# A fused linear-attention and SwiGLU block on one core: the last tile's output split at column 512, and one SwiGLU unit made by halves

## The chip, the core and the metric

The kernel runs on one core of one Trainium2 chip. Time is device time in microseconds (us). The kernel before was run three times: 268.52, 268.66 and 268.88 us, median 268.66. A profiled execution of the same kernel shows every engine: TensorE (PE for its products, PEld for its weight loads, which can overlap the products), VectorE (DVE), ScalarE (ACT), GpSimd (POOL) and SyncE (SP), whose queue issues all the transfers of this kernel.

## The reference

A layer norm of `x` (2048 tokens of 640 features) feeds two branches whose results are added to `x`: a linear attention with a softmax feature map (32 heads of 20 features), and a SwiGLU block of width 1536.

```python
def _A_ref(x, wqkv, w_phi, wo):
    qkv = (x @ wqkv).reshape(B, S, 3, H, Dh).transpose(2, 0, 3, 1, 4)
    q, k, v = qkv[0], qkv[1], qkv[2]
    pq = einsum("bhsd,hdf->bhsf", q, w_phi)
    pk = einsum("bhsd,hdf->bhsf", k, w_phi)
    phi_q = concatenate([softmax(pq), softmax(-pq)], axis=-1)
    phi_k = concatenate([softmax(pk), softmax(-pk)], axis=-1)
    kv = einsum("bhsf,bhsd->bhfd", phi_k, v)
    z  = einsum("bhsf->bhf", phi_k)
    num = einsum("bhqf,bhfd->bhqd", phi_q, kv)
    den = einsum("bhqf,bhf->bhq", phi_q, z)[..., None] + 1e-6
    return (num / den).transpose(0, 2, 1, 3).reshape(B, S, D) @ wo

def _B_ref(x, w1, w3, w2):
    return (silu(x @ w1) * (x @ w3)) @ w2

return x + _A_ref(layernorm(x), ...) + _B_ref(layernorm(x), ...)
```

All arrays are bfloat16.

## The kernel before

Tokens are taken in 16 tiles of 128. The normed input stands transposed in `xnT` (five chunks of 128 features by 2048 tokens). Matrix products accumulate in PSUM, in banks of 512 float32 columns: a pool of six single banks, from which each user takes the next in turn, and one pair. The whole order of work is written out by hand: within one engine's queue, instructions run in the order of the program's text.

The work has three stages.

- A start, in which tiles are loaded, normed and transposed, V is computed, and the weights of the feature map are fused into `wkphi`. Nine of the 48 SwiGLU units are made here, the first two of them in halves by `glu_half`.
- A K stage over 16 tiles: `phi_unit` (products `pk`, L342), the accumulation of `kv` (L485), and two SwiGLU units for a tile, one for the first.
- A Q stage, a loop over t = 0 to 19. While t < 16 it makes `phi_unit` (products `pq`, L342) of tile t. For t = 0 to 3 it makes the last eight SwiGLU units, two for each t, by `fill(2)`. From t = 4 it makes `out_unit` for tile t - 4 and stores the result. `r_unit` (products `pr`, L520) and the division for tile t - 2 stand behind that.

A SwiGLU unit (`glu_unit`, L444) covers 128 of the 1536 hidden features and 512 tokens: five products of 512 columns into the bank `gp` (weights `w1`), five into the bank `up` (weights `w3`). Then ACT takes a Tanh of `gp` (L455), and DVE makes `gs` (L472) and the product for `hT` (L475). `glu_half` (L461) makes one half of a bank, 256 tokens, with five products of 256 columns. `glu_done` starts the Tanh and returns the function that makes the two DVE products.

`out_unit` (products `acc`, L583) makes the output of one tile: 17 rows of weights, 12 from `w2` and 5 from `wo`, each a product with 128 tokens as the stationary operand. For the first 15 tiles the two column halves, 320 each, alternate product by product, and the result is stored by one transfer. For the last tile (`last` is set, t = 19) the columns are done in two parts, one after the other: all 17 products of the first part, its eviction on DVE with the residual added (`result`, L592), its store on SP, and the same for the second part.

Behind the loop stands a branch on every engine (L882): where a bound on the weights isn't met, the attention is made again with the maximum taken off. With these inputs the branch jumps over that part, to the closing barrier (L929), in which SP checks one semaphore after another.

Of the kernel before, what the change touches and what calls it, by code (L numbers as in the profile page):

```python
# [12 lines left out]
def kernel(  # L13
# [24 lines left out]
    _, S, D = A_x.shape  # L38
# [28 lines left out]
    def bank(name, dt=f32):  # L67
        n = 512 if dt == f32 else 1024
        return psum.tile([P, n], dt, name=name, tag="bank")

    def pair(name):
        return psum2.tile([P, 2, 512], f32, name=name, tag="pair")
# [5 lines left out]
    w1 = one.tile([P, KD, F], bf, name="w1")  # L78
    w3 = one.tile([P, KD, F], bf, name="w3")
# [48 lines left out]
    def ld(dst, src):  # L128
        nc.sync.dma_start(out=dst, in_=src)
# [9 lines left out]
    with tc.manual_schedule():  # L139
# [193 lines left out]
        def tile_of(t):  # L333
            return slice(t * P, (t + 1) * P)

        def by_token(cols, w, name, cut, ps=None):

            ps = ps or [bank(name), bank(name)]
            for c in range(KD):
                for i in range(2):  # L340
                    a, b = (0, cut) if i == 0 else (cut, D)
                    nc.tensor.matmul(  # L342
                        ps[i][:, 0 : b - a],
                        xnT[:, c, cols],
                        w[:, c, a:b],
                        start=(c == 0),
                        stop=(c == KD - 1),
                        skip_group_check=True,
                    )
            return ps  # L350
# [45 lines left out]
        def phi_unit(t, w, name, exps=exps, cols=None):  # L396

            ps = by_token(cols or tile_of(t), w, name, CH)
            dst = phi[:, t % 4]
            exps(ps, dst)  # L400
            rows = dst.rearrange("p c g f -> p (c g) f")[:, :, 0:60].rearrange(
                "p a (i d) -> p a i d", d=Dh
            )
            sk = work.tile([P, 2 * NCH, 3], f32, name="sk")
            nc.vector.reduce_sum(out=sk[:], in_=rows, axis=AX.X)  # L405
            rk = work.tile([P, 2 * NCH, 3], f32, name="rk")
            nc.vector.reciprocal(out=rk[:], in_=sk[:])  # L407
            nc.gpsimd.tensor_mul(  # L408
                out=rows, in0=rows, in1=rk[:, :, :, None].to_broadcast([P, 2 * NCH, 3, Dh])
            )  # L410
# [28 lines left out]
        def glu_unit(sc, fi, banks=None):  # L439

            gp, up = banks or (bank("gp")[:], bank("up")[:])
            for ps, w in ((gp, w1), (up, w3)):
                for c in range(KD):
                    nc.tensor.matmul(  # L444
                        ps,
                        w[:, c, fi * P : (fi + 1) * P],
                        xnT[:, c, sc * 512 : (sc + 1) * 512],
                        start=(c == 0),
                        stop=(c == KD - 1),
                    )  # L450
            return glu_done(sc, fi, gp, up)

        def glu_done(sc, fi, gp, up):
            th = work.tile([P, 512], f32, name="th")
            nc.scalar.activation(out=th[:], in_=gp, func=AF.Tanh, scale=0.5)  # L455
            return lambda: glu_product(sc, fi, gp, up, th)

        def glu_half(i, w, sc, fi, ps):

            for c in range(KD):  # L460
                nc.tensor.matmul(  # L461
                    ps[:, i * 256 : (i + 1) * 256],
                    w[:, c, fi * P : (fi + 1) * P],
                    xnT[:, c, sc * 512 + i * 256 : sc * 512 + (i + 1) * 256],
                    start=(c == 0),
                    stop=(c == KD - 1),
                    skip_group_check=True,
                )

        def glu_product(sc, fi, gp, up, th):  # L470
            gs = work.tile([P, 512], bf, name="gs")
            nc.vector.scalar_tensor_tensor(  # L472
                out=gs[:], in0=th[:], scalar=1.0, in1=gp, op0=ALU.add, op1=ALU.mult
            )
            nc.vector.scalar_tensor_tensor(  # L475
                out=hT[:, 4 * sc : 4 * sc + 4, fi, :],
                in0=gs[:].rearrange("p (t s) -> p t s", t=4), scalar=0.5,
                in1=up.rearrange("p (t s) -> p t s", t=4), op0=ALU.mult, op1=ALU.mult,
            )

        def kv_unit(t, v1, acc, first, last):

            for c in range(NCH):
                b, i = divmod(c, 6)
                nc.tensor.matmul(  # L485
                    acc[:, b, VC * i : VC * i + 1 + Dh * HC[c]],
                    phi[:, t % 4, c].rearrange("p g f -> p (g f)"),
                    v1[:, c, 0 : 1 + Dh * HC[c]],
                    start=(first and i == 0),
                    stop=last,  # L490
                    skip_group_check=True,
                )
# [77 lines left out]
        def residual(rows):  # L570
            xr = work.tile([P, D], bf, name="xr")
            ld(xr[:], x2[rows, :])
            return xr

        def out_unit(h, ocols, xr, last=None):

            acc = [bank("acc"), bank("acc")]
            rows = [(h[:, k], w2[:, k]) for k in range(KF)]
            rows += [(oT[:, k, ocols], wo[:, k]) for k in range(KD)]
            res = work.tile([P, D], bf, name="res")  # L580

            def product(j, ps, a, b):
                nc.tensor.matmul(  # L583
                    ps[:, 0 : b - a],
                    rows[j][0],
                    rows[j][1][:, a:b],
                    start=(j == 0),
                    stop=(j == len(rows) - 1),
                )

            def result(ps, a, b):
                nc.vector.tensor_tensor(  # L592
                    out=res[:, a:b], in0=ps[:, 0 : b - a], in1=xr[:, a:b], op=ALU.add
                )

            if last is None:
                parts = [(acc[i], i * HD, (i + 1) * HD) for i in range(2)]
                for j in range(len(rows)):
                    for part in parts:
                        product(j, *part)  # L600
                for part in parts:
                    result(*part)
                return res
            for part in ((acc[0], 0, 384), (acc[1], 384, D)):
                for j in range(len(rows)):
                    product(j, *part)
                result(*part)
                a, b = part[1:]
                ld(out2[last, a:b], res[:, a:b])
# [13 lines left out]
        def flag_unit():  # L623
# [12 lines left out]
        glu = [  # L636
            (sc, fi) for cols in (range(0, 4), range(4, KF)) for sc in range(NSC) for fi in cols
        ]

        def fill(n):  # L640
            for _ in range(n):
                glu_unit(*glu.pop(0))()
# [171 lines left out]
        ps = by_token(tile_of(15), wv, "pv", CH)  # L814
# [6 lines left out]
        acc = pair("pkv")  # L821
# [24 lines left out]
        for t in range(NST + 4):  # L846
            if t < NST:
                phi_unit(t, wqphi, "pq")
            if t < 2:
                kv_unit(turns[t - 2], vaug[:, turns[t - 2]], acc, False, t == 1)  # L850
                if t == 1:
                    kv_done([acc[:, 0], acc[:, 1]])
                    ld(w2, B_w2.rearrange("(c p) d -> p c d", p=P))
            if t < 4:
                fill(2)
            else:
                last = tile_of(NST - 1) if t == NST + 3 else None
                res = out_unit(hT[:, t - 4], tile_of(t % 4), xr, last)
            if 2 <= t < NST + 2:
                r_unit(t - 2)  # L860

            if 3 <= t < NST + 3:
                xr = residual(tile_of(t - 3))
            if 4 <= t < NST + 3:
                ld(out2[(t - 4) * P : (t - 3) * P, :], res[:])
            if t < NST:
                phi_transposed(t)
            if 2 <= t < NST + 2:
                o_transposed(t - 2)
            if t < 4:  # L870
                norm_unit(wqphi, 1, t)
            if t == 4:
                ld(listed[:], norms[:])
                ld(flat, listed[:].rearrange("p g -> (p g)").partition_broadcast(1))
            if t == 6:
                flag_unit()
            if t == 8:
                ok = nc.values_load(flag[0:1, 0:1], min_val=0, max_val=1)
# [3 lines left out]
    with tc.If(ok == 0):  # L882
# [4 lines left out]
        with tc.For_i(0, NST, 1) as t:  # L887
# [3 lines left out]
            acc = pair("pkv")  # L891
# [42 lines left out]
```

## Time and profile before

| what | us |
|---|---|
| median of three runs | 268.66 (268.52 to 268.88) |
| the profiled execution's own time | 268.62 |
| its span, first to last instruction | 266.8 |
| PE busy | 262.0 |
| products of `out_unit`, 320 columns, 299 ns each | 51.3 and 22.8 |
| products of the SwiGLU units, 512 columns, 379 ns each | 57.0 (`up`) and 55.8 (`gp`) |
| weight loads of PEld, 98 ns each | 167.7 in all |
| last eviction on DVE starts | 263.79 |

The duration of a product is from its start to its end, modelled; products overlap, so the step from the start of one to the start of the next is read from groups in the timeline, which give the start of the first and the length of the whole. A few product records are missing from the trace, so that a group can show fewer than it had. In the timeline, "SPq" is SP's queue: the time in which it issues a transfer. "To landing" is the time from that issue to the last semaphore update of the transfer. Register, branch and semaphore instructions are not counted as busy; their times stand in the answers by line.

### The profile page before, as it was taken

How to read it: one execution, taken by the hardware profiler on the slowest of the kernel's cores; microseconds unless marked ns; L12 is line 12 of the kernel's file. 1: busy time of each engine (PE TensorE's matmuls, PEld its weight loads, DVE VectorE, ACT ScalarE, POOL GpSimd, SP SyncE). 2: the span in 40 equal slices, each digit the busy share in tenths (PEclk: the TensorE clock that was granted, in tenths of full speed). 3: DMA queues.
4: the chain of work that ended last, by engine and by line, in shares of the span. 5: the costliest groups of instructions: out<-in, count | busy, mean ns of one | idle time of the engine just before them, and what ended most of it. 6: DMA issues, size and time to landing. Idle time of an engine off the chain costs nothing.

```text
span 266.8 us, 5294 instructions
## 1 busy us (share of the span) xinstructions
PE 262.0 (98%) x1979; PEld 167.7 (63%) x1997; DVE 195.0 (73%) x363; ACT 114.8 (43%) x348; POOL 91.1 (34%) x88
## 2 busy tenths in 40 slices
PE   8999999999999999999999999999999999999995
PEld 7766565655555555555555555677777777777773
DVE  4779984398766777779998699976877777776341
ACT  5784444744466666344556665422222222221000
POOL 5052520055333333333444333333344444333000
PEclk9999999999999999999999999999999999999999
DMA  6998856976000000060000098455655555556931
GB/s 192 248 245 185 125 118 160 333 136 119 0 0 2 0 1 3 1 176 0 0 2 0 0 270 179 114 142 144 130 128 133 149 130 128 137 147 130 155 98 55
DMA packets 69373, 29.46 MB, mean 110 GB/s; under 512 B 56287, under 2 KB 67935, under 8 KB 69344
## 3 DMA queue, kind: packets, MB, share of 16 engines
q1 hardware_dynamic: 69344, 29.08, 46.9%
q8 instruction: 17, 0.28, 0.4%
q14 instruction: 12, 0.10, 0.2%
HBM read 13.14 MB, written 2.63 MB: 59 GB/s over the span
## 4 chain that ended last, share of the span: by engine, by line
PE 98%; issue 0%; DVE 0%
PE acc L583 28%; PE up L444 19%; PE gp L444 18%; PE pq L342 8%; PE pk L342 8%; PE pv L342 6%; PE pr L520 2%; PE pkv L485 2%; PE pv L299 2%; PE pf L428 1%; PE idle L202 1%; PE pst L288 1%; PE g L461 1%; PE v L299 1%; PE gp L461 0%; PE up L461 0%
## 5 line engine op out<-in xcount | busy, mean ns | idle before, releaser
L408 POOL TENSOR_TENSOR phi<-phi,rk 128x1320 bf16<-128x1320 bf16 x32 | 77.2, 2412 | 129.0 <-DVE rk L407 102.3
L444 PEld LDWEIGHTS <-w 128*128 128x128 bf16 x460 | 43.4, 98 | 47.9 <-DMA w<-in_B_w_dram 0.2
L405 DVE TENSOR_REDUCE sk<-phi 128x66 f32<-128x1320 bf16 x32 | 48.8, 1526 | 26.7 <-ACT phi L371 25.7
L444 PE MATMUL up<-xnT,w 128*128 128x512 bf16 x227 | 57.0, 379 | 0.3
L444 PE MATMUL gp<-xnT,w 128*128 128x512 bf16 x215 | 55.8, 378 | 0.7
L583 PE MATMUL acc<-reg_v,reg_h 128*128 128x320 bf16 (+2 forms) x384 | 54.9, 299 | 0.0
L342 PEld LDWEIGHTS <-xnT 128*128 128x128 bf16 x440 | 41.7, 98 | 19.3 <-DMA xnT<-reg_h 0.5
L371 ACT ACTIVATE phi<-pq 128x360 bf16<-128x360 f32 (+2 forms) x96 | 24.8, 366 | 57.7 <-issue 34.6
L583 PEld LDWEIGHTS <-reg_h 128*128 128x128 bf16 x384 | 37.4, 98 | 14.4
L455 ACT ACTIVATE th<-gp 128x512 f32<-128x512 f32 x47 | 28.4, 603 | 27.9 <-PE gp L444 25.7
L475 DVE SCALAR_TENSOR_TENSOR reg_h<-gs,up 128x512 bf16<-128x512 bf16 x47 | 32.3, 688 | 4.8
L472 DVE SCALAR_TENSOR_TENSOR gs<-th,gp 128x512 bf16<-128x512 f32 x47 | 30.9, 658 | 4.3 <-ACT th L455 4.3
L371 ACT ACTIVATE phi<-pk 128x360 bf16<-128x360 f32 (+2 forms) x96 | 24.9, 370 | 20.0 <-PE pk L342 20.0
L592 DVE TENSOR_TENSOR res<-acc,xr 128x320 bf16<-128x320 f32 (+2 forms) x32 | 14.2, 484 | 19.0 <-PE acc L583 19.0
L583 PE MATMUL acc<-reg_w,reg_v 128*128 128x320 bf16 (+2 forms) x160 | 24.5, 299 | 0.0
L342 PE MATMUL pk<-wkphi,xnT 128*128 128x360 bf16 (+1 forms) x160 | 24.3, 299 | 0.0
L342 PE MATMUL pq<-wqphi,xnT 128*128 128x360 bf16 (+1 forms) x160 | 24.3, 299 | 0.0
L407 DVE RECIPROCAL rk<-sk 128x66 f32<-128x66 f32 x32 | 18.1, 567 | 3.2
L583 PEld LDWEIGHTS <-reg_v 128*128 128x128 bf16 x160 | 15.7, 98 | 6.1
L342 PE MATMUL pv<-reg_w,xnT 128*128 128x360 bf16 x120 | 17.4, 299 | 0.0
L228 DVE BATCH_NORM_STATS2 st<-reg_h 128x6 f32<-128x320 bf16 x32 | 13.4, 477 | 4.1 <-DMA reg_h<-in_A_x_dram 4.1
L541 DVE TENSOR_TENSOR o__77<-pr,den 128x360 bf16<-128x360 f32 (+1 forms) x32 | 14.2, 486 | 0.6
(82 smaller groups left out, 162.4 us busy)
## 6 DMA issues: line engine op xcount, KB each, us to landing
w<-in_B_w_dram SPq DMA_DIRECT2D x2, 1280.0 KB, 6.3
xr<-in_A_x_dram SPq DMA_DIRECT2D x16, 160.0 KB, 2.4
out_dram<-res SPq DMA_DIRECT2D x15, 160.0 KB, 1.8
reg_h<-in_A_x_dram SPq DMA_DIRECT2D x6, 320.0 KB, 4.7
reg_v<-in_B_w_dram SPq DMA_DIRECT2D x1, 1920.0 KB, 9.2
w<-in_B_w_dram SPq DMA_DIRECT2D x4, 320.0 KB, 4.4
reg_w<-in_A_wqkv_dram SPq DMA_DIRECT2D x5, 160.0 KB, 3.1
reg_w<-in_A_wo_dram SPq DMA_DIRECT2D x1, 800.0 KB, 7.2
```

What stands on the lines that cost most here:

```text
L342: nc.tensor.matmul(ps[i][:, 0 : b - a], xnT[:, c, cols], w[:, c, a:b], start=(c == 0), stop=(c == KD - 1), skip_group_check=True,)
L371: nc.scalar.activation(out=dst[:, c0 : c0 + n, g, 0:k], in_=p.rearrange("p (c f) -> p c f", c=n), func=AF.Exp, scale=1.0 - 2.0 * g,)
L405: nc.vector.reduce_sum(out=sk[:], in_=rows, axis=AX.X)
L407: nc.vector.reciprocal(out=rk[:], in_=sk[:])
L408: nc.gpsimd.tensor_mul(out=rows, in0=rows, in1=rk[:, :, :, None].to_broadcast([P, 2 * NCH, 3, Dh]))
L444: nc.tensor.matmul(ps, w[:, c, fi * P : (fi + 1) * P], xnT[:, c, sc * 512 : (sc + 1) * 512], start=(c == 0), stop=(c == KD - 1),)
L455: nc.scalar.activation(out=th[:], in_=gp, func=AF.Tanh, scale=0.5)
L472: nc.vector.scalar_tensor_tensor(out=gs[:], in0=th[:], scalar=1.0, in1=gp, op0=ALU.add, op1=ALU.mult)
L475: nc.vector.scalar_tensor_tensor(out=hT[:, 4 * sc : 4 * sc + 4, fi, :], in0=gs[:].rearrange("p (t s) -> p t s", t=4), scalar=0.5, in1=up.r ...
L541: nc.vector.tensor_mul(out=o_[:, t % 2, Dh * h0 : Dh * h1].rearrange("p (h d) -> p h d", d=Dh), in0=p3[:, :, 0:20], in1=den[:, h0:h1, None ...
L583: nc.tensor.matmul(ps[:, 0 : b - a], rows[j][0], rows[j][1][:, a:b], start=(j == 0), stop=(j == len(rows) - 1),)
L592: nc.vector.tensor_tensor(out=res[:, a:b], in0=ps[:, 0 : b - a], in1=xr[:, a:b], op=ALU.add)
```

## The change

Two places are edited. The last tile's two parts become columns 0 to 512 and 512 to 640, in place of 0 to 384 and 384 to 640; both stores are still issued by SP. In the Q stage, at t = 0, the second of the two SwiGLU units is made by a new function, which makes each of the two banks in two halves of 256 tokens: 20 products of 256 columns with 20 weight loads, in place of 10 products of 512 columns with 10 weight loads. The order of all other instructions on every engine is the same; PE's program has 20 instructions more.

```diff
+        def glu_by_halves(sc, fi):
+
+            gp, up = bank("gp")[:], bank("up")[:]
+            for ps, w in ((gp, w1), (up, w3)):
+                for i in range(2):
+                    glu_half(i, w, sc, fi, ps)
+            glu_done(sc, fi, gp, up)()
+
...
-            for part in ((acc[0], 0, 384), (acc[1], 384, D)):
+            for part in ((acc[0], 0, 512), (acc[1], 512, D)):
                 for j in range(len(rows)):
                     product(j, *part)
                 result(*part)
...
             if t < 4:
-                fill(2)
+                fill(1)
+                if t == 0:
+                    glu_by_halves(*glu.pop(0))
+                else:
+                    fill(1)
             else:
```

The new function's `glu_half` is the one of the start, unchanged. Lines of the changed kernel from `glu_by_halves` on are 8 to 12 higher than those of the kernel before: `product` is L591, `result` L600, the branch L894 and the barrier L941.

## The prediction

> **What bounds the kernel now.** I read three views in this order: the busy table of the page, the chain that ended last in order of time, and the timeline of the last 8 us.
>
> ```profile
> PE 262.0 (98%) x1979; PEld 167.7 (63%) x1997; DVE 195.0 (73%) x363; ACT 114.8 (43%) x348; POOL 91.1 (34%) x88
> ```
>
> ```profile
> 146.46 1.08 PE gp L444 x5
> 147.54 1.08 PE up L444 x5
> ...
> 254.51 9.26 PE acc L583 x68
> 263.77 0.02 issue
> 263.79 0.42 DVE res L592
> ```
>
> TensorE (PE) is busy for 262.0 of 266.8 us, and the chain is PE from the first product to 263.77. In the Q stage one unit follows the other without a hole: gp and up of the first SwiGLU unit of t = 0 take 1.08 us each. So whatever PE does more or less in this stage goes straight to the end; nothing covers it. After the last product there is a tail in which PE no longer counts.
>
> ```profile
> 258.97 2.11 PE L583 MATMUL acc<-reg_v,reg_h 128*128 128x384 bf16 x12
> 261.73 1.47 PE L583 MATMUL acc<-reg_v,reg_h 128*128 128x256 bf16 x12
> 261.93 0.56 DVE L592 TENSOR_TENSOR res<-acc,xr 128x384 bf16<-128x384 f32 x1 [2.01 <-PE acc L583]
> 263.04 0.71 PE L583 MATMUL acc<-reg_w,reg_v 128*128 128x256 bf16 x5
> 263.79 0.42 DVE L592 TENSOR_TENSOR res<-acc,xr 128x256 bf16<-128x256 f32 x1 [1.30 <-PE acc L583]
> ```
>
> ```profile
> 264.24 0.33 SPq L129 DMA_DIRECT2D out_dram<-res  x1
> ```
>
> ```profile
> L882 SPq EVENT_SEMAPHORE  x4: 17/17/17, 265.1 to 265.4; - x4
> L882 PEldq COMPARE_BRANCH  x1: 3617/3617/3617, 261.6 to 261.6; - x1
> L882 SPq COMPARE_BRANCH  x1: 53/53/53, 264.6 to 264.6; - x1
> ```
>
> The tail is: eviction (264.21), issue of the second store on SP (264.24 to 264.57), SP's branch around the fallback (264.63), then a row of semaphore checks on SP, 60 to 80 ns apart without a hole, to 265.97, and the closing barrier. In the trace's records by semaphore, the check on PE stands at 265.85 and was met since 265.33; the check on the second store stands at 265.91 and its last part had landed at 265.76. Neither held SP. So the end follows SP's last issue by 2.55 us, and that issue follows the last eviction. The slacks, 0.51 us for PE's branch and 0.15 us for the store, are what a change can use up.
>
> **The change, part by part.**
>
> *The unit by halves.* Ten 512-column products become twenty of 256. A run of five 512-column products takes 1.08 us, 216 ns each. 256 columns: the last part's first to thirteenth product start 263.04 - 261.73 = 1.31 us apart, 12 steps, 109.2 ns. The half products at the start of the kernel (L461) step by the same. 20 x 109.2 - 10 x 216 = +24 ns on PE. All twenty weight loads lie under the products, as they do there. The buffers, the Tanh and the two DVE products are the same, released when the last half of gp or up is done; that moves with those 24 ns only. No range is needed: the same shape with the same operands stands in the trace.
>
> *The last tile on PE.* 17 x 384 + 17 x 256 columns become 17 x 512 + 17 x 128. Before: the first part steps by (261.73 - 258.97) / 17 = 162.4 ns. After: 17 x 216 = 3.67 us, then 16 steps of 128 columns to the last product's start. The nearest row for 128 columns at full clock is the transposes of one tile early on:
>
> ```profile
> 12.79 0.44 PE L288 MATMUL pst<-ident,reg_h 128*128 128x128 bf16 x5
> 13.07 0.71 PE L461 MATMUL gp<-xnT,w 128*128 128x256 bf16 x5
> ```
>
> Five in 0.28 us, 56 ns each. The last product so starts at 258.97 + 0.024 + 3.67 + 16 x 0.056 = 263.565 against 263.480 before: +85 ns with the halves. It lasts 219 ns (median of the 128-column row of L288) in place of 273: -54 ns. Bounds: 54 ns (a third of the 162.4 of 384 columns) to 109 (no gain over 256 columns, +0.85 us); I take 56, since the 63-column products of L520, each with its own weight load, run eleven in 0.33 us, 30 ns each, so no weight load holds them at more than that.
>
> The Trainium skill, TensorE: Matmul & The Clock Gate, Back-to-back issue gap, speaks against this: it gives about 81 ns for 128 columns in a stream of weight loads and products, and 131 for 512. By that the sixteen steps would take 16 x 25 = 0.40 us more than by the row, an estimate. The trace disagrees at both ends that it has (216 ns at 512 columns, 30 ns at 63).
>
> *The evictions.* 256 columns took 424 ns, 384 took 558: 1.05 ns a column. So 128 columns take 290 (-134 ns) and 512 take 692. The first part's last product starts at 262.45 and ends 0.38 later at 262.83 (378 ns is the 512-column mean), its eviction ends at 263.56, and the last product at 263.78: DVE is free by 0.22 us. Were it not, the last eviction would wait for the rest.
>
> *The stores on SP.* The first store, 128 KB, is issued at 263.58 to 263.92 in place of 262.52; the second is ready when the last eviction ends, 263.82 + 0.29 = 264.11 against 264.21. SP is free by 0.2 us. No wait is added; behind the second store SP has only its branch and the checks.
>
> Landing of the second store, 32 KB in rows of 256 bytes:
>
> ```profile
> out_dram<-res SPq DMA_DIRECT2D x1, 96.0 KB, 2.4
> out_dram<-res SPq DMA_DIRECT2D x1, 64.0 KB, 1.5
> listed<-norms SPq DMA_DIRECT2D x1, 4.0 KB, 1.6
> ```
>
> Between 1.5 (512-byte rows) and 1.6 us (32-byte rows) by the two nearest, 2.4 at worst; up to 1.67 stays hidden behind SP's checks. The packets of the first store should be gone: those of the 96 KB started 0.83 us after issue and all but one engine's ran 0.3 us, so here 264.41 to about 264.8, while the second's start near 264.95.
>
> *Sum.* +24 (halves) +61 (last products' start) -54 (last product) -134 (last eviction) = -103 ns. 266.79 - 0.10 = 266.69 us of span. The profiled execution took 268.62 with 1.83 us around its span, so 268.52; it stands 0.04 below the median of the runs, 268.66. Forecast: 268.56.
>
> **Rivals.**
>
> *PE's branch becomes the last to arrive (slower).* It went out at 261.59, when the last 34 loads and products were still queued, and ended 3.62 us later. With 128-column products the last 34 are shorter: it goes out at about 262.45. If its 3.62 us run from there, PE reports at 266.07 + 0.12 = 266.19, where SP checks at 265.75: it decides from a PE report later than that. The end comes 0.44 - 0.10 = +0.34 us, 269.00. For it: ACT's branch and GpSimd's, whose engines had little queued, show 1.4 and 2.5 us from branch to next instruction with an instruction packet in flight between; DVE's and SP's, without one, some 0.5. PE had such a packet of 16 KB at 262.86 to 263.78. Against: the twenty extra instructions also move PE's branch relative to those packets, of which 17 served some 4,000 PE instructions, one for every 240 or so; a packet fetched before the branch would leave it about 0.5 us, and then PE reports well before the check. If the 3.62 us is instead the drain of PE (1.46 us after its last product), nothing moves.
> The Trainium skill, Runtime: NRT & Kernel Launch, Instruction fetch mechanics, says that blocks of 16 KiB are fetched in sequence and that a taken branch out of the held blocks waits for a fetch; the packets' size and spacing agree, which side of a block boundary the branch falls on no row shows.
>
> *The small store lands late.* At 1.8 us (median of the full stores) it lands at 265.93, past the check at 265.81: +0.02, 268.68. At 2.4, the 96 KB store's: 266.5, +0.6, 269.26. For it: the two stores are now 0.53 us apart on one queue in place of 1.72. Against: its size, and the 96 KB store was late on one engine only, shared with the instruction packet.
>
> *The weight loads become PE's bound (slower).* A load lasts 98 ns in PEld's rows, which the 109 ns of a half product covers and the 56 ns of 128 columns doesn't. If each product had to wait for its own load, the sixteen steps cost 16 x (98 - 56) = 0.67 us more: -0.10 + 0.67 = +0.57, 269.23. Against: the 30 ns of L520 and the 56 of L288, both under the 98 of their loads. The page on TensorE named above points this way with its 81 ns.
>
> *More is gained outside the span.* PE's next instruction packet starts at 265.94 and ends 0.58 us past the span's end. If the 1.83 us around the span wait for it and an earlier branch brings it forward, up to 0.58 us more: about 268.0.
>
> **How the numbers follow.** Forecast 0.55, range 268.4 to 268.75 by the spread of the runs shown (0.36 us). Branch 0.18, late store 0.12 (0.09 small, 0.03 large), weight loads 0.04, more outside 0.11. 0.2% is 0.54 us, about what a measurement of this kernel can tell from no change: under 268.12 is faster, over 269.20 slower. Faster takes most of the last rival and a little of the forecast, 0.12; slower takes the large late store, the weight loads and a little of the branch, 0.10; the rest, 0.78, is within. The range, 268.15 to 269.05, holds the forecast, the branch, the small late store and the nearer half of the last.
>
> **What would show it.** The unit of L461 in the Q stage at 2.18 us against 2.16; 128-column products of L591 56 ns apart; the last eviction 0.29 us and ending near 264.11; SP's last issue 0.10 earlier and its checks without a hole. The forecast is wrong if a gap opens before SP's check on PE (branch) or on the last store, or if the 128-column products step at over 60 ns.

## The result, and the profile after

The changed kernel takes 269.92 us (median of 12 runs, 268.99 to 270.55) against 268.55 of the kernel before on the same chip: 1.37 us more. The ratio is 1.0047, 95% interval 1.0035 to 1.0059. The forecast was 268.56 in 268.15 to 269.05; it was wrong. The profiled execution took 269.67 us.

The page of the changed kernel, its head and the busy table:

```profile
span 268.0 us, 5332 instructions
...
PE 261.9 (98%) x2007; PEld 167.1 (62%) x2007; DVE 194.8 (73%) x363; ACT 114.8 (43%) x348; POOL 91.2 (34%) x88
```

The span is 1.2 us longer and PE's busy time is the same: the loss is where PE has nothing to do. (Two of the twelve times, 268.99 and 269.17 us, lie half a microsecond below the other ten; no trace was taken of such an execution.) The chain of the changed kernel around the edited unit, and the timeline of its end:

```profile
147.04 1.08 PE up L444 x5
148.12 1.09 PE gp L461 x10
149.21 1.09 PE up L461 x10
```

```profile
258.49 2.75 PE L591 MATMUL acc<-reg_v,reg_h 128*128 128x512 bf16 x12
262.16 0.83 PE L591 MATMUL acc<-reg_v,reg_h 128*128 128x128 bf16 x12
262.36 0.69 DVE L600 TENSOR_TENSOR res<-acc,xr 128x512 bf16<-128x512 f32 x1 [2.92 <-PE acc L591]
262.83 0.44 PE L591 MATMUL acc<-reg_w,reg_v 128*128 128x128 bf16 x5
263.31 0.29 DVE L600 TENSOR_TENSOR res<-acc,xr 128x128 bf16<-128x128 f32 x1 [0.26 <-PE acc L591]
```

The halved unit takes 2.18 us, a whole one 2.16. The 128-column products step by 0.67 / 12 = 56 ns (262.16 to 262.83), and the last eviction takes 0.29 us. All of that is as forecast. (The last product ends 0.48 us earlier than in the execution of before, because this execution was already 0.51 us ahead at the first `pq`, 144.27 against 144.78. The lead comes from the start, which the edit doesn't touch: there the same products ran faster, five of L288 in 0.44 us from 3.96 where before they took 0.74 from 4.12. So ends are compared below from the last product on.) What comes behind is not as forecast. SP's last issue, SP's waits in the last 8 us, and the landings of the last two stores in the changed kernel:

```profile
263.62 0.33 SPq L129 DMA_DIRECT2D out_dram<-res  x1
```

```profile
SPq L941 <- DMA out_dram<-res: 1.8, 1, 1.8
```

```profile
out_dram<-res SPq DMA_DIRECT2D x1, 128.0 KB, 1.7
out_dram<-res SPq DMA_DIRECT2D x1, 32.0 KB, 3.4
```

The small store was issued on time and took 3.4 us to land, where the 64 KB store of before took 1.5. SP stood 1.8 us in front of its check on it. By the trace's records, 15 of the store's 16 parts had landed by 265.07; the last came at 267.07. Two windows of the transfers in the changed kernel, 264.67 to 266.05 and 266.0 to 266.4, tell why (each queue's packets, their MB, and the share that they took of all 16 engines):

```profile
q8 instruction: 1, 0.02, 6.2%
q14 instruction: 1, 0.01, 3.4%
q1 hardware_dynamic: 8, 0.00, 0.7%
```

```profile
DMA packets 9, 0.00 MB, mean 5 GB/s; under 512 B 9, under 2 KB 9, under 8 KB 9
...
q1 hardware_dynamic: 9, 0.00, 6.0%
```

One packet of 16 KB on the queue q8, PE's instructions, holds 6.2% of sixteen engines, that is one engine, through the whole of the first window. The 9 packets of the second window are the 8 of 256 bytes that this engine owes the store (128 rows / 16) and the semaphore write behind them; they move as soon as the big packet is done. (Of the 8 in the first window, 7 are the last of the other engines' shares, before 264.73, and one is the first of the held ones, at 266.03.) So one sixteenth of the store waits for a block of PE's program. The packet records don't name the engine; that it is the same one is read from the times. In all three traces in which the last store is held (this one and two below, "PE late" and the second of the halves alone), its held packets start to move 0.014 us before the recorded end of q8's packet. The 8 KB packet on q14 isn't what holds them: here it ends at 265.96, and in the trace of "PE late" at 267.23, where they move from 267.53. The packet on q8 is the one that follows PE's branch. In the kernel before there is one too, in the window 265.9 to 267 of that trace:

```profile
DMA packets 1, 0.02 MB, mean 15 GB/s; under 512 B 0, under 2 KB 0, under 8 KB 0
...
q8 instruction: 1, 0.02, 8.1%
```

It is alone there: at 265.94 everything had landed. PE came to it later, as the branch shows. The lines are those of PE's sequencer: the branch lasts until PE leaves it, and the semaphore behind it is PE's report to SP (changed kernel; before the branch lasted 3617 ns, with the semaphore at 265.3):

```profile
L894 PEldq COMPARE_BRANCH  x1: 1845/1845/1845, 262.0 to 262.0; - x1
L894 PEldq EVENT_SEMAPHORE  x1: 51/51/51, 263.9 to 263.9; - x1
```

From the last product's end to the end of the span it is 3.04 us before and 4.70 after: -0.13 us (the second store is issued 0.36 us after the last product, before it was 0.49) +1.78 us (SP's check on that store, met at 267.07 in place of 265.29). The span grew by less, 1.2 us, because of the 0.48 us by which this execution was ahead.

### The profile page after: what moved, and what is told of

The parts are those of the page before. It is cut to its first block, busy times and chain, and to the rows that moved or that the text cites. A ratio compares the mean times of both kernels' runs of the same rounds, so it can differ in the third digit from the quotient of the medians.

```text
span 268.0 us, 5332 instructions
## 1 busy us (share of the span) xinstructions
PE 261.9 (98%) x2007; PEld 167.1 (62%) x2007; DVE 194.8 (73%) x363; ACT 114.8 (43%) x348; POOL 91.2 (34%) x88
## 4 chain that ended last, share of the span: by engine, by line
PE 95%; DMA 2%; SPq 1%; issue 0%; DVE 0%
PE acc L591 28%; PE up L444 18%; PE gp L444 18%; PE pq L342 8%; PE pk L342 8%; PE pv L342 6%; PE pr L528 2%; PE pkv L493 2%; DMA reg_h<-in_A_x_dram 2%; SPq L129 1%; PE pf L428 1%; PE pv L299 1%; PE up L461 1%; PE gp L461 1%; PE g L461 1%; PE pst L288 0%
## 5 line engine op out<-in xcount | busy, mean ns | idle before, releaser
L444 PEld LDWEIGHTS <-w 128*128 128x128 bf16 x450 | 42.3, 97 | 46.9 <-DMA w<-in_B_w_dram 0.4
L444 PE MATMUL up<-xnT,w 128*128 128x512 bf16 x225 | 55.9, 379 | 0.0
L591 PE MATMUL acc<-reg_v,reg_h 128*128 128x320 bf16 (+2 forms) x384 | 54.9, 299 | 0.0
L591 PEld LDWEIGHTS <-reg_h 128*128 128x128 bf16 x384 | 36.9, 98 | 15.0
L600 DVE TENSOR_TENSOR res<-acc,xr 128x320 bf16<-128x320 f32 (+2 forms) x32 | 14.2, 484 | 18.8 <-PE acc L591 18.8
L591 PE MATMUL acc<-reg_w,reg_v 128*128 128x320 bf16 (+2 forms) x160 | 24.5, 299 | 0.0
L591 PEld LDWEIGHTS <-reg_v 128*128 128x128 bf16 x160 | 15.5, 98 | 6.3
```

What stands on the lines that cost most here:

```text
L444: nc.tensor.matmul(ps, w[:, c, fi * P : (fi + 1) * P], xnT[:, c, sc * 512 : (sc + 1) * 512], start=(c == 0), stop=(c == KD - 1),)
L591: nc.tensor.matmul(ps[:, 0 : b - a], rows[j][0], rows[j][1][:, a:b], start=(j == 0), stop=(j == len(rows) - 1),)
L600: nc.vector.tensor_tensor(out=res[:, a:b], in0=ps[:, 0 : b - a], in1=xr[:, a:b], op=ALU.add)
```

## The experiments

Three theories stood against one another. A: PE's instruction packets meet the stores on one DMA engine, and the number of instructions in PE's program decides when. B: a store of 256-byte rows half a microsecond behind another lands late by itself. C: the unit by halves costs the time. Each timed kernel was run beside the kernel before on the same chip, whose median was 269.01 us for the first four and 268.60 for the rest.

### The split alone

```diff
-            for part in ((acc[0], 0, 384), (acc[1], 384, D)):
+            for part in ((acc[0], 0, 512), (acc[1], 512, D)):
```

(against the kernel before)

> The kernel before with the split at 512 alone, no unit by halves. Theory A (the 16 KB packet of PE's program that follows its branch meets the second store on one DMA engine; when it comes is set by how many instructions stand in PE's program before the branch): PE's own packet before the branch starts about 1.3 us after the branch goes out, PE leaves the branch 1.4 us after that packet's end, some 3.5 us after the branch went out, and the next packet comes after the second store has landed. The second store lands in 1.4 to 1.6 us; SP waits instead for PE's report, some 0.3 to 0.5 us. Time -0.1 to +0.5 us against before. Theory B (a 32 KB store of 256-byte rows, half a microsecond behind the first, lands late by itself): the second store takes 3 us or more as in the changed kernel, +1.0 to +1.7 us. Theory C (the unit by halves costs the time): -0.1 us.

Measured: 269.31 us, ratio 1.0010 (0.9999 to 1.0020). B falls: the store lands in 1.9 us, not in 3 or more, and 0.5 of that is a longer issue. (That issue also puts it later behind the first store than in the changed kernel; the kernels without the branch, below, have it at the same distance.) PE's branch and SP's last issue in this kernel:

```profile
L882 PEldq COMPARE_BRANCH  x1: 3564/3564/3564, 263.2 to 263.2; - x1
L882 PEldq EVENT_SEMAPHORE  x1: 51/51/51, 266.8 to 266.8; - x1
```

```profile
264.86 0.84 SPq L129 DMA_DIRECT2D out_dram<-res  x1
```

The issue takes 0.84 us in place of 0.33. Here the packet that PE's branch itself asks for lies at 264.22 to 265.31, on the packets of the first store, and SP's issue of the second is done 0.38 us after that packet. Against C it speaks weakly: A's range holds the interval (-0.03 to +0.54 us), C's -0.1 us lies just below it. PE's report (266.88) would have come 0.4 us after SP's check, had SP not been held up itself: the check stood at 266.97, 0.50 us late.

### The halves alone

```diff
-            for part in ((acc[0], 0, 512), (acc[1], 512, D)):
+            for part in ((acc[0], 0, 384), (acc[1], 384, D)):
```

(against the changed kernel)

> The changed kernel with the split back at 384, the unit by halves kept. Theory A: PE leaves its branch about 1.5 us earlier than in the kernel before, the next packet starts near the packets of the second store (64 KB), and meets them on one engine in most executions: +0.2 to +1.5 us against before, the second store landing in 1.9 to 3.4 us. Theory B: 0.0 to +0.05 us, the second store in 1.5 us. Theory C: +1.0 to +1.7 us with the second store in 1.5 us and the loss elsewhere.

> A second look at the split at 384 with the unit by halves, whose twelve times fell in two groups, 268.6 to 269.1 and 269.9 to 270.9 us, and whose trace was of the first. Theory A: where the time is of the second group, PE's own packet has started before its branch goes out, and the packet after the branch meets the second store (64 KB), which lands in 2.5 to 3.5 us; where it is of the first, the trace is as before. Theory B: the second store lands in 1.5 us in both.

Measured: 269.94 us, ratio 1.0028 (1.0010 to 1.0046), in two groups: five runs at 268.55 to 269.07, seven at 269.89 to 270.85. Two traces were taken: the first is of an execution of 268.64 us, as the lower group, the second of one of 270.36, as the upper. PE's branch in the first, then in the second, and what SP waited for at the end and how the last store landed in the second:

```profile
L894 PEldq COMPARE_BRANCH  x1: 3520/3520/3520, 261.7 to 261.7; - x1
```

```profile
L894 PEldq COMPARE_BRANCH  x1: 2285/2285/2285, 262.3 to 262.3; - x1
```

```profile
SPq L941 <- DMA out_dram<-res: 1.2, 1, 1.2
```

```profile
out_dram<-res SPq DMA_DIRECT2D x1, 64.0 KB, 2.9
```

The first has no such wait, a tail of 3.04 us as the kernel before, and the 64 KB store in 1.5 us. In the second that store lands in 2.9. So the same program shows both, and a store of 64 KB is caught as one of 32 KB is: where PE leaves its branch early, the next packet (265.30 to 266.74) falls on the store. It also ends C: in the lower group the halves cost nothing that can be seen.

### Ten instructions more, and forty

```diff
-            for ps, w in ((gp, w1), (up, w3)):
-                for i in range(2):
-                    glu_half(i, w, sc, fi, ps)
+            for i in range(2):
+                glu_half(i, w1, sc, fi, gp)
+            for c in range(KD):
+                nc.tensor.matmul(up, w3[...], xnT[...], ...)
```

(against the changed kernel; the arguments of the product are shortened to "...")

> The changed kernel with only the gate bank of that unit by halves: 10 instructions more than the kernel before in place of 20, split at 512. Theory A: PE's own packet before the branch starts about 1.1 us later than in the changed kernel, PE leaves the branch that much later, about 1.2 us after its last product, still ahead of SP's check, and the next packet starts only when the second store has landed: -0.15 to +0.1 us against before. Theory B: +1.0 to +1.7 us. Theory C: half of the changed kernel's loss, +0.5 to +0.8 us.

Measured: 269.37 us, ratio 1.0013 (1.0003 to 1.0023), that is +0.08 to +0.62 us. B falls again; C's +0.5 to +0.8 isn't excluded by this time, and A's -0.15 to +0.1 is missed by the median. A's place was wrong: PE's own packet wasn't moved by ten instructions; it starts 1.03 us after the branch goes out, as with the split alone, and meets the first store. SP's issue takes 1.12 us.

```diff
-                fill(1)
-                if t == 0:
-                    glu_by_halves(*glu.pop(0))
-                else:
-                    fill(1)
+                for _ in range(2):
+                    if t == 0:
+                        glu_by_halves(*glu.pop(0))
+                    else:
+                        fill(1)
```

(against the changed kernel)

> The changed kernel with both units of t = 0 by halves: 40 instructions more than the kernel before. Theory A (packets of PE's program meet the stores): PE's own packet comes some 2 us earlier than in the changed kernel and no longer holds the branch; if PE then leaves the branch without waiting for its queue to empty, the packet after the branch comes 1 us or more earlier too and meets the first store in place of the second, as the packet before the branch did in the kernels with 0 and 10 instructions more: SP's issue of the second store takes 0.8 to 1.2 us in place of 0.33, +0.2 to +0.7 us against before. If PE leaves the branch only about when its products end, the second store is met as in the changed kernel, +1.0 to +1.7 us. Theory B (the small, close second store is late by itself): +1.0 to +1.7 us whatever the packets do. Theory C (the halves cost the time): twice the changed kernel's loss, +2 to +3 us.

Measured: 269.26 us, ratio 1.0027 (1.0017 to 1.0037), that is +0.46 to +0.99 us: a smaller loss than the changed kernel's, with twice its halves, so C's +2 to +3 falls. PE's branch with forty instructions more, SP's last issue, and the transfers from 264.2 to 265.2:

```profile
L894 PEldq COMPARE_BRANCH  x1: 460/460/460, 262.5 to 262.5; - x1
L894 PEldq EVENT_SEMAPHORE  x1: 51/51/51, 263.9 to 263.9; - x1
```

```profile
264.17 1.37 SPq L129 DMA_DIRECT2D out_dram<-res  x1
```

```profile
q1 hardware_dynamic: 136, 0.12, 36.0%
q8 instruction: 1, 0.02, 6.0%
```

PE's own packet had ended 1.07 us before the branch went out and holds it no more: the branch takes 0.46 us. The packet after it comes at 264.21 and now falls on the first store. SP's second issue takes 1.37 us, somewhat over the 0.8 to 1.2 that A expected, and is again done 0.37 us after the packet.

### PE kept busy behind its last product

```diff
+            tail = pair("tail")
+            for _ in range(4):
+                nc.tensor.matmul(tail[:, 0], nought[:], xnT[:, 0, 0:512])
```

(against the changed kernel)

> The changed kernel with four products of 512 columns (0.86 us) behind PE's last real product, into a bank that nobody reads; no eviction or store waits for them. Theory A, if PE leaves its branch only when its queue is empty: the packet after the branch starts 0.86 us later, behind the landing of the second store: -0.15 to +0.1 us against before. If PE leaves the branch 1.4 us after the end of its own packet whatever is queued, the packet is not moved or comes a little earlier, and the loss stays, +0.5 to +1.7 us. Theory B: +1.0 to +1.7 us. Theory C: the same.

Measured: 270.16 us (six runs), ratio 1.0047 (1.0029 to 1.0066): the loss stays whole. In this kernel's trace SP waits for the same store, as long as in the changed one:

```profile
SPq L944 <- DMA out_dram<-res: 1.8, 1, 1.8
```

PE's queue was busy to 265.66, and PE left its branch at 265.35. So the branch doesn't wait for the queue to empty, and work behind the last product doesn't move the packet.

### Without the branch

Both kernels without `with tc.If(ok == 0)` and the fallback behind it; with these inputs the fallback isn't run.

> The kernel before without the branch and the fallback behind it (with these inputs the fallback isn't run; the flag is still computed). SP has no branch of 0.5 us between its last issue and its checks, and PE no packet after a branch. All theories: -0.3 to -0.8 us against before, and it is the base for the next kernel.

> The changed kernel (split at 512, one unit by halves) without the branch and the fallback. Theory A: no packet comes behind a branch, the second store lands in 1.4 to 1.7 us, and the kernel is within -0.3 to +0.2 us of the kernel with the split at 384 without the branch. Theory B: the second store still lands in 3 us or more, +1.0 to +1.7 us against that kernel. Theory C: the same loss with the store in time.

Measured: the split at 384 takes 268.46 us, ratio to the kernel before 0.9992 (0.9982 to 1.0002); the changed kernel 268.25, ratio 0.9990 (0.9977 to 1.0004). So without the branch the change costs nothing: 0.21 us less by the medians, within their noise, where -0.10 was forecast for the whole kernel. The last two stores of the changed kernel without the branch:

```profile
out_dram<-res SPq DMA_DIRECT2D x1, 128.0 KB, 1.7
out_dram<-res SPq DMA_DIRECT2D x1, 32.0 KB, 1.4
```

The same small store, behind the same first one, with the same halves on PE, lands in 1.4 us. This settles it against B and C: the store is late only where the packet is. The kernel with the split at 384 was to gain 0.3 to 0.8 us by all theories, and that was wrong by size: it gained 0.14 by the medians (the interval reaches from a gain of 0.48 to a loss of 0.05). SP, without its branch, now comes to the check of the second store before it has landed, and waits:

```profile
SPq L902 <- DMA out_dram<-res: 0.8, 1, 0.8
```

### All of it in one table

From the trace's records, in us from the end of the last real product. "Own" is the packet before PE leaves its branch, "next" the one after it; SP's issue is that of the second store.

| kernel | more instr. | own packet | PE leaves branch | next packet | SP's issue | span's end |
|---|---|---|---|---|---|---|
| before | 0 | -0.89 to 0.03 | 1.46 | 2.19 to 3.61 | 0.33 | 3.04 |
| split alone | 0 | -0.28 to 0.81 | 2.26 | 3.00 to 3.95 | 0.84 | 3.41 |
| ten more | 10 | -0.27 to 1.10 | 2.54 | 3.30 to 4.26 | 1.12 | 3.69 |
| halves, first trace | 20 | -1.14 to -0.06 | 1.36 | 2.19 to 3.50 | 0.33 | 3.04 |
| halves, second trace | 20 | -2.40 to -1.31 | 0.12 | 0.88 to 2.32 | 0.33 | 4.24 |
| changed | 20 | -2.16 to -0.89 | 0.54 | 1.40 to 2.78 | 0.33 | 4.70 |
| PE late | 28 | -2.25 to -0.87 | 0.56 | 1.30 to 2.75 | 0.33 | 4.68 |
| forty more | 40 | -3.62 to -2.38 | -0.85 | 0.40 to 1.36 | 1.37 | 3.94 |
| 384, no branch | 0 | none | - | none | 0.33 | 2.89 |
| 512, no branch | 20 | -2.11 to -0.96 | - | none | 0.33 | 2.69 |

In the first seven rows PE leaves its branch 1.42 to 1.44 us after its own packet's end. The two rows without a branch tell where that packet comes from: with no more instructions none is fetched near the end, with twenty more one is fetched in sequence, 2.11 us before the last product's end, where the changed kernel has it. So without those instructions it is the branch that asks for the packet (1.03 to 1.27 us after it goes out); with them the running program has asked before, in three of the four traces with twenty more and in those with 28 and 40. So A holds for the packet and the store; that the number of instructions alone decides when the packet comes isn't borne out, since with twenty more one and the same program shows both.

The table also gives a price. In the eight traces in which a packet holds a part of a store (the first eight rows), the held part landed 1.0 to 1.2 us after the packet's end.

## Why the prediction was wrong

- *What bounds the kernel; the unit by halves; the last tile on PE; the evictions.* Right: 2.18 us for the unit, 56 ns a product, 291 and 691 ns for the evictions where 290 and 692 stood. The second store was issued 0.132 us sooner after the last product (0.356 against 0.488 us), where 0.134 was forecast for the eviction. The 81 ns of the Trainium skill, TensorE: Matmul & The Clock Gate, Back-to-back issue gap, is not what the stream of loads and products shows here.
- *"Between 1.5 and 1.6 us by the two nearest, 2.4 at worst; up to 1.67 stays hidden".* This is the step that failed. The small store took 3.45 us from issue. The 1.5 us was the time of a store that no instruction packet had met, and it holds only for such a one: without the packet the small store lands in 1.4. The 2.4 us was the time of a store whose parts began to move at 263.35, when the packet had 0.43 us left to run. The prediction named that cause (one engine, shared with the packet), but set it against a late store, as if the packet belonged to the 96 KB store. And 2.4 wasn't the worst: the small store's parts began at 264.46, and its packet came at 264.67 and ran for 1.37 us.
- *The branch.* The prediction saw that the twenty instructions move PE's own packet, and said that PE then reports well before SP's check. It does: 263.93 against a check at 265.23 (its branch took 1.85 us, not 0.5, because the packet had started only 0.86 us before it). The prediction took an early report for harmless. But PE goes through its branch earlier, and the packet after the branch comes earlier too, from 2.19 us behind the last product to 1.40, on the second store. The rival on gains outside the span even looked at this following packet, and counted its coming forward as a gain only. No such gain shows: the time around the span is 1.70 us in the changed kernel and 1.83 before, and 1.70 to 1.84 in all ten traces, whether the packet ends inside the span or behind it. A term was missing: what else lies on the DMA engines at the new time.
- *The rival in which PE's branch holds the end.* Its mechanism is real, though not in this kernel: with the split alone PE left its branch 3.56 us after it went out. There it is covered by SP's longer issue.
- *The late store as a rival* had the right place, SP's check on the second store, and +0.6 us at most, with 0.03 for it. It cost 1.78 us in the profiled execution; the medians lose 1.37 in all.

## What to carry to other kernels

A block of an engine's own program is a transfer too: here 16 KB on one DMA engine for 0.9 to 1.5 us, and a store has a part on each engine, so the store ends when the slowest engine does. In the last microseconds, where nothing covers a store, find these packets in the trace and ask where each lands after the edit; here twenty instructions, added some 115 us ahead of the last product, moved one. A slack of 0.15 us in front of a check is no cover, and a duration read from a row holds only while the row's neighbours stay away.

## What the runs showed of the hardware

- An instruction packet of 16 KB lasted 0.9 to 1.5 us near the end of these traces, and the packets of a store on the same engine didn't move until it was done (256-byte packets from 266.03, its end 266.05; in the kernel before, 768-byte packets from 263.77, its end 263.78).
- The hold reaches SP: in the three kernels in which a packet still lies on the first store when SP issues the second, that issue lasts 0.84, 1.12 and 1.37 us in place of 0.33, and is done 0.37 to 0.38 us after the packet's end.
- Where a packet was asked for by PE's branch, the branch cost 1.03 to 1.27 us to the start of the packet, the packet, and 1.43 us more; with the packet there 1.07 us before it, 0.46 us. The Trainium skill, Runtime: NRT & Kernel Launch, Instruction fetch mechanics, has fetches in sequence and a stall at a branch whose target isn't held; the kernel with the split at 512 and no branch (a packet 2.11 us before the last product's end) and the one with forty instructions more (0.46 us) agree.
- One program can show two times: the split at 384 with the halves fell into two groups, with medians of 268.70 and 270.12 us; the ends of its two traces, counted from the last product, are 1.20 us apart. The two traces differ in whether the packet was fetched before the branch went out. What decides that from one execution to the next was not tried.
